# Attention and MLP on one core: the diagonals of the softmax sums move off GpSimd, and their product with ones moves in TensorE's order

## The chip, the cores and the metric

The kernel runs on one core of one Trainium2 chip. A core has TensorE (PE in the profile; PEld is its weight load), VectorE (DVE), ScalarE (ACT), GpSimd (POOL) and SyncE (SP), each with an instruction queue of its own that it works off in order, and DMA engines that move data between HBM and on-chip memory. The metric is the device time of one execution, in microseconds. Lower is better.

## The reference

Sliding-window attention with four sink positions, then a two-layer MLP. All inputs are float32.

```python
# q, k, v: [4, 8, 768, 64] (batch, heads, sequence, head size); 4 sinks, window 128
scores = matmul(q, k.T) / sqrt(64)
keep   = (pos_k < 4) | ((0 <= pos_q - pos_k) & (pos_q - pos_k < 128))
scores = where(keep, scores, -1e9)
a      = exp(scores - max(scores))
a      = a / (sum(a) + 1e-9)
x      = matmul(a, v)                        # then [3072, 512]: heads side by side
h      = x @ w_in                            # [512, 2048]
g      = where(h >= 1, h, where(h <= -1, 0, (h + 1)**2 / 4))
out    = g @ w_out                           # [2048, 512]
```

The factors on q and k (about 30) make the softmax sharp, so that the scores need float32's precision.

## The kernel before

**Tiles and chunks.** A unit is 384 query positions (CT = 3 tiles of 128) of one head of one batch; there are 64. Eight units, the heads of one batch and one half of the sequence, make a chunk, whose rows are then 384 tokens of the MLP. The program records steps: the attention of one chunk is interleaved (`spread`) with the MLP of the chunk before. TensorE keeps the recorded order (`manual_schedule` for PE). On the other engines a scheduler that goes by a modelled timeline sets the order, so that a change at one place moves instructions elsewhere too.

**Two kinds of attention.** The first 16 units (NATIVE) are worked in 8 pairs of heads, with float32 matmuls (`pair_*`). The other 48 go one by one with values split in two parts of a shorter format (`scores`, `transp`, `av`); the change doesn't touch these. Nor does it touch the MLP (`stage1`, `stage2`), which has split values too.

**A pair.** For pair m, `pair_scores(m, i)` multiplies q by k for query tile i and both heads, adds the mask and takes the maximum on VectorE (line 388), and makes exp on ScalarE (line 393), which also sums each row into `stat`. After the third tile (line 395 on), the sums are finished: 1e-9 is added on GpSimd (line 396), VectorE takes the reciprocal (397), and GpSimd multiplies the identity by it, a column of 128 per query tile (400): `diag` is three diagonal matrices of 128 x 128 beside each other, and lives in a buffer named q_l. One step later `pair_r` multiplies `diag` by a matrix of ones (437), which puts one over the sum of each query into every row of a PSUM bank; ScalarE copies that into `xn` (438). `early_transp` turns the unnormalized p (408, 410) and ScalarE copies it out (411, 412, 414). `pair_av` multiplies it by v (427), and VectorE multiplies the result by `xn` (430). So the division comes last, and no instruction ahead of `pair_av` needs `diag`.

**Steps.** `pair_steps(m)` holds what belongs to pair m and to pair m - 1 at once: three scores of pair m (sc), four half transposes of pair m - 1 (tp: both parts of head a, then of head b), then the product with ones and p times v of pair m - 1 (pv). For m that is a multiple of 4 the order of these differs a little. In what follows, step m is this list; step 4 has pair 4's scores and pair 3's p times v. Steps 0 to 4 are the first chunk, with no MLP beside them but the decoding of four weight tiles; steps 5 to 8 are interleaved with the first chunk's MLP and the decoding of the other twelve.

**Decoding.** The weights come as 64-bit words of float64 (lines 150 to 156). VectorE puts the bits together with three instructions (150, 153, 154), ScalarE rounds to the high part (155), VectorE subtracts for the rest (156). 16 tiles (8 of `w_in`, 8 of `w_out`) of 1 MB each are loaded by SyncE's queue, later by ScalarE's (173).

**PSUM.** `ps_a` has three banks, which scores, transposes, the product with ones and p times v share in turn.

Of the kernel before, what the change touches and what calls it, by code (L numbers as in the profile page):

```python
# [12 lines left out]
AF = mybir.ActivationFunctionType  # L13
ALU = mybir.AluOpType

B, H, S, D = 4, 8, 768, 64
DM, DFF = 512, 2048
P = 128
NT = S // P
CT = 3  # L20
# [29 lines left out]
def attn_ffn(ctx, tc, qk, qkp, vx, vs, par, w_in, w_out, out):  # L50
    nc = tc.nc
# [10 lines left out]
    ident = const.tile([P, P], F32, name="ident")  # L62
# [57 lines left out]
    for r0 in (0, 32):  # L120
        r = r0 + CT * NSINK
# [226 lines left out]
    def pair_load(m):  # L348

        b, h, _ = units[2 * m]  # L350
        T = CT * P
        W = CT * KB - NSINK
        q_s = att.tile([P, T], F32R, name="q_h").bitcast(F32)
        k_s = att.tile([P, P + CT * KB], F32R, name="k_s").bitcast(F32)[:, :W]
        loaded.append(nc.sync.dma_start(k_s, qkp[b, h // 2, :, T:T + W]).ins)
        nc.sync.dma_start(q_s, qkp[b, h // 2, :, 0:T])
        st["qk", m] = q_s, k_s

    def pair_values(m):
        v_s = vq[m % 2]  # L360
        for a in range(2):
            b, h, _ = units[2 * m + a]
            nc.sync.dma_start(v_s[:, :CT, a], vx[b, h, :, :CT])
            nc.sync.dma_start(v_s[:NSINK, CT, a], vs[b, h, :NSINK])

    def early_p(u):

        return (p0[u % 2] if u // 2 % 2 == 0 else pt0[u % 2][:, 5 * P:5 * P + CT * 260]).rearrange(
            "p (i c) -> p i c", c=260)

    def pair_scores(m, i):
        q_s, k_s = st["qk", m]
        lo, c0 = (KB if i == 0 else 0), max(0, (i - 1) * KB)
        banks = []
        for a in range(2):

            pool, name = ((ps_o, "o_ps"), (ps_o, "o_ps"), (ps_o, "o_ps"), (ps_h, "h_ps"), (ps_h, "h_ps"),
                          (ps_a, "ps_a"))[2 * i + a] if m <= H // 2 - 1 else (ps_a, "ps_a")
            ps = pool.tile([P, 512], F32, name=name)
            r = slice(a * D, a * D + D)  # L380
            nc.tensor.matmul(ps[:, lo:260], lhsT=q_s[r, i * P:(i + 1) * P], rhs=k_s[r, c0:c0 + 260 - lo],
                             start=True, stop=True)
            banks.append(ps)
        for a, ps in enumerate(banks):
            u = 2 * m + a
            p = early_p(u)[:, i, lo:260]
            peak_i = peak[:, u, i:i + 1]
            nc.vector.tensor_tensor_reduce(out=p, in0=ps[:, lo:260], in1=(m0, m1n, m2)[i], scale=-0.125, scalar=3.0e38,
                                           op0=ALU.add, op1=ALU.min, accum_out=peak_i)
            if not i:  # L390
                st["sum", u] = att.tile([P, 2 * CT], F32, name=f"stat{a}")
            stat = st["sum", u]
            nc.scalar.activation(p, p, AF.Exp, bias=peak_i, scale=-1.0, accum_out=stat[:, i:i + 1])
            if i == CT - 1:

                nc.gpsimd.tensor_scalar(stat[:, CT:2 * CT], stat[:, 0:CT], 1.0e-9, None, op0=ALU.add)
                nc.vector.reciprocal(stat[:, CT:2 * CT], stat[:, CT:2 * CT])  # L397
                diag = st["diag", u] = att.tile([P, CT * P], F32R, name="q_l").bitcast(F32)
                for n in range(CT):
                    nc.gpsimd.tensor_scalar(diag[:, n * P:(n + 1) * P], ident, stat[:, CT + n:CT + n + 1], None,  # L400
                                            op0=ALU.mult)

    def early_transp(u, part):

# [27 lines left out]
    def pair_r(m):  # L432

        T = CT * P
        ps = ps_a.tile([P, 512], F32, name="ps_a")
        for a in range(2):
            nc.tensor.matmul(ps[a * D:a * D + D, :T], lhsT=ones, rhs=st.pop(("diag", 2 * m + a)), start=True, stop=True)  # L437
        nc.scalar.copy(xn[:, units[2 * m][1] // 2, :], ps[:, :T])

    def pair_steps(m):  # L440

        a, b = 2 * m - 2, 2 * m - 1
        sc = [(0.45, lambda i=i: pair_scores(m, i)) for i in range(CT)] if m < NATIVE // 2 else [(0.0, lambda: None)] * CT
        steps = [(0.0, lambda: pair_load(m + 1))] if m + 1 < NATIVE // 2 else []
        if m < NATIVE // 2:
            steps.append((0.0, lambda: pair_values(m)))
        if not m:
            return [(0.0, lambda: pair_load(0))] + steps + sc
        tp = [(0.35, lambda u=u, i=i: early_transp(u, i)) for u in (a, b) for i in range(2)]
        pv = [(0.65, lambda: pair_r(m - 1)), (1.2, lambda: pair_av(m - 1))]  # L450
        if m % (H // 2) == 0:
            return steps + tp[:3] + sc[:1] + pv[:1] + tp[3:] + sc[1:2] + pv[1:] + sc[2:]
        return steps + tp[:1] + sc[:1] + tp[1:3] + pv[:1] + tp[3:] + sc[1:2] + pv[1:] + sc[2:]

# [195 lines left out]
    with tc.If(other_v > 0):  # L652
        with tc.tile_pool(name="gen", bufs=1) as gen:

            for n in range(2 * NJ):
# [3 lines left out]
                m = gen.tile([P, DM], F32, name="m")  # L659
# [3 lines left out]
            for t0 in (0, CT):  # L663
                keep = gen.tile([P, CT, S], F32, name="keep")
                kidx = gen.tile([P, S], I32, name="kidx")
                r = gen.tile([P, S], F32, name="r")
                for i in range(CT):
                    m = keep[:, i]
# [53 lines left out]
```

## Time and profile before

| | |
|---|---|
| median of 3 runs | 761.11 us (760.46 to 762.45) |
| the profiled execution | 761.86 us |
| its span, first to last instruction | 759.9 us |
| mean granted TensorE clock | 0.973 |
| busy: TensorE, VectorE, ScalarE, GpSimd | 708.2, 517.0, 492.2, 357.8 us |

A row of a group of instructions reads: line, engine, operation, tile written <- tiles read, shapes, count | busy us, mean ns of one | idle us of the engine ahead of them, and what ended it. A row of the waits reads: who waited <- for whom: us in total, times, longest. A row of the table by stages reads: stretch in us from the start, its length, each engine's busy time with its count of instructions, granted TensorE clock, share of the DMA engines, GB/s. A row of the timeline reads: start, duration, engine, line, operation, tiles, shapes, count [idle before it <- what ended that]. A row of the chain reads: start, duration, engine, tile, line, count. A row on one line of the kernel gives the shortest, the median and the longest duration in ns.

### The profile page before, as it was taken

What the parts mean: (1) busy time and instruction counts of PE and PEld (TensorE: products, weight loads), DVE (VectorE), ACT (ScalarE), POOL (GpSimd) and SP (SyncE); (2) the same over time, 40 slices, a digit from 0 to 9 for tenths busy, and PEclk for the clock granted to TensorE, in tenths of its full rate; (3) what the DMA queues carried; (4) which work ended last, traced back from release to release, by engine and by line L of the source; (5) the groups of instructions that cost most, each with busy time, mean ns of one, the idle gap of its engine ahead of it and who ended that gap; (6) DMA issues with size and microseconds to landing.
All of it is one profiled execution on the core that took longest, in us unless ns stands there. A gap on an engine that the chain in (4) does not pass through costs nothing.

```text
span 759.9 us, 12272 instructions
## 1 busy us (share of the span) xinstructions
PE 708.2 (93%) x3873; PEld 613.0 (81%) x3873; DVE 517.0 (68%) x1321; ACT 492.2 (65%) x1265; POOL 357.8 (47%) x578
## 2 busy tenths in 40 slices
PE   4667997889999999999999999999999999999996
PEld 2234765678999899999988999899988999999985
DVE  6345877666877678777878778787888677742221
ACT  3445655466777787778877787678867676644342
POOL 5334547657545255564656555564656455410000
PEclk9768998999999999999999999999999999999999
DMA  7714333131313253333333344333332121001001
GB/s 224 232 47 166 137 136 122 66 103 43 97 54 107 69 151 114 117 120 134 117 97 115 85 143 141 95 120 132 117 93 65 53 87 46 9 1 43 1 0 47
DMA packets 44841, 73.04 MB, mean 96 GB/s; under 512 B 13024, under 2 KB 29408, under 8 KB 44768
## 3 DMA queue, kind: packets, MB, share of 16 engines
q1 hardware_dynamic: 41504, 59.59, 25.8%
q10 hardware_dynamic: 3264, 12.58, 4.6%
q8 instruction: 33, 0.54, 0.3%
q14 instruction: 40, 0.33, 0.1%
HBM read 65.87 MB, written 6.29 MB: 95 GB/s over the span
## 4 chain that ended last, share of the span: by engine, by line
PE 68%; POOL 9%; DVE 9%; issue 5%; DMA 4%; ACT 4%; SPq 0%; POOLq 0%; ACTq 0%
PE o_ps L503 27%; PE h_ps L484 27%; POOL q_l L400 6%; PE ps_a L342 4%; PE ps_a L240 4%; PE ps_a L295 2%; PE ps_a L427 1%; PE ps_a L437 1%; DVE k_s L224 1%; DMA w<-w_in 1%; DVE p L259 1%; POOL gl L495 1%; POOL q_l L226 1%; DVE gl L495 1%; DVE bits L153 1%
## 5 line engine op out<-in xcount | busy, mean ns | idle before, releaser
L484 PE MATMUL h_ps<-x,wi 128*128 128x384 f32 x1536 | 311.1, 341 | 1.3 <-DVE g L493 1.3
L484 PEld LDWEIGHTS h_ps<-x,wi 128*128 128x128 f32 x1536 | 264.1, 189 | 13.0 <-issue 3.3
L503 PE MATMUL o_ps<-w,gh 128*128 128x512 f32 x768 | 245.1, 400 | 0.4 <-ACT gh L494 0.4
L503 PE MATMUL o_ps<-w,gl 128*128 128x512 f32 x384 | 152.1, 396 | 0.4 <-POOL gl L495 0.4
L503 PEld LDWEIGHTS o_ps<-w,gh 128*128 128x128 f32 x768 | 135.0, 189 | 17.5 <-issue 2.0
L493 DVE SCALAR_TENSOR_TENSOR g<-g,h_ps 128x384 f32<-128x384 f32 x128 | 70.2, 549 | 65.5 <-ACT g L492 64.7
L491 ACT ACTIVATE g<-h_ps,half 128x384 f32<-128x384 f32 x128 | 73.8, 577 | 62.4 <-PE h_ps L484 62.1
L226 POOL TENSOR_TENSOR q_l<-r,q_h 128x384 fp32r<-128x384 f32 x48 | 50.1, 1043 | 128.1 <-ACT q_h L225 111.2
L494 ACT CAST gh<-g 128x384 fp32r<-128x384 f32 x128 | 65.5, 512 | 55.7 <-DVE g L493 54.8
L503 PEld LDWEIGHTS o_ps<-w,gl 128*128 128x128 f32 x384 | 72.5, 189 | 18.6 <-POOL gl L495 0.8
L495 DVE TENSOR_TENSOR gl<-g,gh 128x384 fp32r<-128x384 f32 x112 | 69.2, 618 | 24.4 <-ACT gh L494 23.4
L247 ACT ACTIVATE p<-p,peak 128x260 f32<-128x260 f32 (+1 forms) x144 | 71.3, 496 | 15.2 <-DVE peak L244 14.3
L224 DVE TENSOR_TENSOR k_s<-k_r,k_s 64x524 fp32r<-64x524 f32 (+1 forms) x44 | 47.1, 1071 | 43.5 <-ACT k_s L222 43.4
L244 DVE CUSTOM_DVE_ANT_0 p<-ps_a,m 128x260 f32<-128x260 f32 (+1 forms) x144 | 57.3, 409 | 17.1 <-PE ps_a L240 16.0
L492 ACT ACTIVATE g<-g 128x384 f32<-128x384 f32 x128 | 67.0, 524 | 2.6
L306 POOL TENSOR_SCALAR_AFFINE_SELECT pt<-pt 128x384 fp32r<-128x384 f32 (+1 forms) x96 | 50.8, 529 | 24.5 <-DVE pt L299 21.3
L304 POOL TENSOR_SCALAR_AFFINE_SELECT pt<-pt 128x384 fp32r<-128x384 f32 (+1 forms) x96 | 51.5, 537 | 7.2 <-ACT pt L298 3.2
L259 DVE TENSOR_SCALAR p<-p,stat 128x132 f32<-128x132 f32 (+1 forms) x144 | 51.6, 412 | 0.1
L400 POOL TENSOR_SCALAR q_l<-ident,stat 128x128 f32<-128x128 f32 x48 | 47.2, 998 | 4.2 <-DVE stat L397 2.8
L342 PEld LDWEIGHTS ps_a<-pt,v_s 128*128 128x128 f32 x304 | 46.4, 188 | 2.3
L342 PE MATMUL ps_a<-pt,v_s 128*128 128x256 f32 (+1 forms) x304 | 46.7, 273 | 0.0
L240 PE MATMUL ps_a<-k_s,q_h 128*128 128x260 f32 (+1 forms) x144 | 40.1, 279 | 3.2 <-DVE sk L301 2.4
(148 smaller groups left out, 1033.7 us busy)
## 6 DMA issues: line engine op xcount, KB each, us to landing
r<-qk SPq DMA_DIRECT2D x48, 192.0 KB
k_r<-qk SPq DMA_DIRECT2D x32, 262.0 KB
again<-w_in SPq DMA_DIRECT2D x16, 512.0 KB
again<-w_out SPq DMA_DIRECT2D x16, 512.0 KB
w<-w_in ACTq DMA_DIRECT2D x6, 1024.0 KB
w<-w_out ACTq DMA_DIRECT2D x6, 1024.0 KB
out<-o SPq DMA_DIRECT2D x23, 256.0 KB
r<-vx SPq DMA_DIRECT2D x32, 128.0 KB
```

The costliest lines, as they stand in the source:

```text
L240: nc.tensor.matmul(ps[:, lo:260], lhsT=q[:, i * P:(i + 1) * P], rhs=k_s[:, c0:c0 + 260 - lo], start=(j == 0), stop=(j == len(qs) - 1))
L247: nc.scalar.activation(p[:, i, lo:260], p[:, i, lo:260], AF.Exp, bias=peak_i, scale=-1.0, accum_out=stat[:, i:i + 1])
L259: nc.vector.tensor_scalar(p[:, i, lo:260], p[:, i, lo:260], stat[:, CT + i:CT + i + 1], None, op0=ALU.mult)
L342: nc.tensor.matmul(z, lhsT=w, rhs=y, start=(n == 0), stop=(n == len(mms) - 1))
L400: nc.gpsimd.tensor_scalar(diag[:, n * P:(n + 1) * P], ident, stat[:, CT + n:CT + n + 1], None, op0=ALU.mult)
L484: nc.tensor.matmul(h_ps[:, :T], lhsT=w_i[j][:, w, ct * P:(ct + 1) * P], rhs=x[:, y, ct], start=(ct == 0 and n == 0), stop=(ct == NCT - 1 a ...
L491: nc.scalar.activation(g, h_ps[:, :T], AF.Relu, bias=half, scale=0.5)
L492: nc.scalar.activation(g, g, AF.Square)
L493: nc.vector.scalar_tensor_tensor(g, g, 1.0, h_ps[:, :T], op0=ALU.min, op1=ALU.max)
L494: nc.scalar.copy(gh, g)
L495: (nc.gpsimd if row0 == GL_POOL else nc.vector).tensor_tensor(gl, g, gh.bitcast(F32), op=ALU.subtract)
L503: nc.tensor.matmul(o_ps[tt], lhsT=gg[:, tt * P:(tt + 1) * P], rhs=w_o[j][:, w], start=(j == 0 and n == 0), stop=(j == NJ - 1 and n == 2))
```

## The change

The addition of 1e-9 moves from GpSimd to VectorE. For pairs 0 to 3, VectorE makes the three diagonals of a head in one instruction, the identity and the reciprocals being read broadcast. For pairs 4 to 7, ScalarE makes them, as three copies with a scale. In TensorE's order the product with ones is put behind the last transpose, and outside of steps 4 and 8 behind the second score too.

```diff
             if i == CT - 1:
 
-                nc.gpsimd.tensor_scalar(stat[:, CT:2 * CT], stat[:, 0:CT], 1.0e-9, None, op0=ALU.add)
-                nc.vector.reciprocal(stat[:, CT:2 * CT], stat[:, CT:2 * CT])
+                r = stat[:, CT:2 * CT]
+                nc.vector.tensor_scalar(r, stat[:, 0:CT], 1.0e-9, None, op0=ALU.add)
+                nc.vector.reciprocal(r, r)
                 diag = st["diag", u] = att.tile([P, CT * P], F32R, name="q_l").bitcast(F32)
-                for n in range(CT):
-                    nc.gpsimd.tensor_scalar(diag[:, n * P:(n + 1) * P], ident, stat[:, CT + n:CT + n + 1], None,
-                                            op0=ALU.mult)
+                if m < H // 2:
+                    nc.vector.tensor_tensor(diag.rearrange("p (i q) -> p i q", q=P),
+                                            ident.unsqueeze(1).broadcast_to([P, CT, P]),
+                                            r.unsqueeze(2).broadcast_to([P, CT, P]), op=ALU.mult)
+                else:
+                    for n in range(CT):
+                        nc.scalar.activation(diag[:, n * P:(n + 1) * P], ident, AF.Copy, scale=r[:, n:n + 1])
...
         if m % (H // 2) == 0:
-            return steps + tp[:3] + sc[:1] + pv[:1] + tp[3:] + sc[1:2] + pv[1:] + sc[2:]
-        return steps + tp[:1] + sc[:1] + tp[1:3] + pv[:1] + tp[3:] + sc[1:2] + pv[1:] + sc[2:]
+            return steps + tp[:3] + sc[:1] + tp[3:] + pv[:1] + sc[1:2] + pv[1:] + sc[2:]
+        return steps + tp[:1] + sc[:1] + tp[1:] + sc[1:2] + pv + sc[2:]
```

The new lines move those behind them: line numbers from 400 on grow by 5 (408 becomes 413, 437 becomes 442, 427 becomes 432, 430 becomes 435, 484 becomes 489).

TensorE in step 2, before: the second part of head a's transposes, the first of head b's, the product with ones, then the second part of head b's, the scores of tile 1, and p times v (vq is v, spn the sinks' part of p).

```order
L408 MATMUL ps_a<-ident,pt 128x128 x2
L410 MATMUL ps_a<-ident,pt 4x128
L408 MATMUL ps_a<-ident,pt 128x128 x3
L437 MATMUL ps_a<-q_l,ones 64x384 x2
L408 MATMUL ps_a<-ident,pt 128x128 x2
L410 MATMUL ps_a<-ident,pt 4x128
L381 MATMUL o_ps<-k_s,q_h 128x260
L381 MATMUL h_ps<-k_s,q_h 128x260
L427 MATMUL ps_a<-pt,vq_166 64x128 x2
```

And now:

```order
L413 MATMUL ps_a<-ident,pt 128x128 x2
L415 MATMUL ps_a<-ident,pt 4x128
L413 MATMUL ps_a<-ident,pt 128x128 x5
L415 MATMUL ps_a<-ident,pt 4x128
L381 MATMUL o_ps<-k_s,q_h 128x260
L381 MATMUL h_ps<-k_s,q_h 128x260
L442 MATMUL ps_a<-q_l,ones 64x384 x2
L432 MATMUL ps_a<-pt,vq_166 64x128 x2
```

The product with ones (L437, now L442) has gone behind three transposes and two scores, and stands directly ahead of p times v.

VectorE in the same step, before: from the softmax of the last tile of pair 1's second head to the first softmax of pair 2's tile 1 (ISA is the mask with its maximum, and the read of the maximum; bits are the words being decoded).

```order
L388 ISA pt_178,peak_97<-ps_a_312,m2_106 128x260
L388 ISA peak_97 128x1
L397 RECIPROCAL stat0_257<-stat0_257 128x3
L388 ISA p_175,peak_97<-o_ps_343,m0_109 128x128
L388 ISA peak_97 128x1
L154 SCALAR_TENSOR_TENSOR bits1_304<-w_203,bits1_304 128x1024
L388 ISA p_176,peak_97<-o_ps_345,m0_109 128x128
L388 ISA peak_97 128x1
L397 RECIPROCAL stat1_260<-stat1_260 128x3
L156 TENSOR_TENSOR w_303<-bits1_304,w_303 128x2x512
L388 ISA p_175,peak_97<-o_ps_374,m1n_108 128x260
```

And now, from the two additions on:

```order
L397 TENSOR_SCALAR stat0_253<-stat0_253 128x3
L397 TENSOR_SCALAR stat1_256<-stat1_256 128x3
L154 SCALAR_TENSOR_TENSOR bits1_300<-w_203,bits1_300 128x1024
L388 ISA p_175,peak_97<-o_ps_362,m1n_108 128x260
L388 ISA peak_97 128x1
L398 RECIPROCAL stat0_253<-stat0_253 128x3
L398 RECIPROCAL stat1_256<-stat1_256 128x3
L388 ISA p_176,peak_97<-h_ps_364,m1n_108 128x260
L388 ISA peak_97 128x1
L401 TENSOR_TENSOR q_l_314<-ident_79,stat0_253 128x384
L401 TENSOR_TENSOR q_l_320<-ident_79,stat1_256 128x384
L156 TENSOR_TENSOR w_299<-bits1_300,w_299 128x2x512
```

The two diagonals now stand behind the third decode instruction and the softmax of both heads' tile 1.

ScalarE at the start of the MLP, now (L496 is the first activation of an MLP tile, L419, L416 and L417 copy transposes out):

```order
L393 ACTIVATE p,stat_529<-p,peak 128x260
L173 DMA w<-w_out 128x2x1024
L393 ACTIVATE pt,stat_618<-pt,peak 128x128
L393 ACTIVATE pt,stat_621<-pt,peak 128x128
L406 ACTIVATE q_l<-ident,stat_526 128x128 x3
L406 ACTIVATE q_l<-ident,stat_529 128x128 x3
L496 ACTIVATE g<-h_ps,half 128x384
L416 COPY pt<-ps_a 128x256
```

The six diagonals of pair 4 (L406) stand between two exponentials of pair 5 and the first MLP activation, which before followed the exponentials directly.

## The prediction

> **What bounds the kernel now.** I began with the page: the busy shares, the chain of work that ended last, and the group on GpSimd's diagonals.
>
> ```profile
> PE 708.2 (93%) x3873; PEld 613.0 (81%) x3873; DVE 517.0 (68%) x1321; ACT 492.2 (65%) x1265; POOL 357.8 (47%) x578
> PEclk9768998999999999999999999999999999999999
> PE o_ps L503 27%; PE h_ps L484 27%; POOL q_l L400 6%; PE ps_a L342 4%; PE ps_a L240 4%; PE ps_a L295 2%; PE ps_a L427 1%; PE ps_a L437 1%; DVE k_s L224 1%; DMA w<-w_in 1%; DVE p L259 1%; POOL gl L495 1%; POOL q_l L226 1%; DVE gl L495 1%; DVE bits L153 1%
> L400 POOL TENSOR_SCALAR q_l<-ident,stat 128x128 f32<-128x128 f32 x48 | 47.2, 998 | 4.2 <-DVE stat L397 2.8
> ```
>
> TensorE is busy for 93% of the span, so only the missing 7%, some 50 us, and the time at a low clock can be won. GpSimd's 47.2 us of diagonals are mostly on the chain (6% of the span, some 42 us), though GpSimd as a whole is the least busy engine. Next, by stage, the waits of TensorE (first up to 72 us, then 72 to 190 us), and the table of stages, cut where TensorE begins a pair:
>
> ```profile
> PE ps_a L437 <- POOL q_l L400: 17.8, 8, 3.7
> PE ps_a L437 <- POOL q_l L400: 8.7, 5, 2.9
> PE h_ps L484 <- DVE g L493: 1.3, 1, 1.3
> core 0: us, PE busy (x) PEld busy (x) DVE busy (x) ACT busy (x) POOL busy (x), PEclk, DMA share, GB/s
> 8.66:24.16 15.50, 10.93 (x45) 5.17 (x45) 7.99 (x27) 7.76 (x27) 6.11 (x9) 1.00 0.71 230
> 24.16:40.93 16.77, 9.74 (x46) 4.43 (x44) 7.23 (x22) 6.73 (x22) 7.13 (x9) 0.69 0.71 226
> 40.93:57.24 16.31, 10.41 (x47) 4.74 (x45) 7.22 (x21) 6.70 (x22) 6.57 (x8) 0.69 0.14 37
> 57.24:71.67 14.43, 9.68 (x46) 4.69 (x44) 7.96 (x21) 6.93 (x22) 5.73 (x8) 0.76 0.33 106
> 71.67:160.20 88.53, 78.52 (x418) 58.77 (x419) 62.37 (x108) 49.62 (x121) 50.44 (x48) 0.96 0.35 122
> 190.00:720.00 530.00, 526.49 (x2971) 480.80 (x2970) 389.27 (x1033) 379.44 (x975) 256.54 (x442) 1.00 0.30 90
> ```
>
> Two stages carry the case. From 8.7 to 71.7 us four pairs run alone (steps 1 to 4): no engine is full, and each step is one chain. From 71.7 to 160 us four more pairs run between the first chunk's MLP matmuls: TensorE is nearly full there and waits 8.7 us for the diagonals. Behind 190 us TensorE is full, and no instruction of the change is left; I put that part at nothing. The timeline of step 2 shows the chain:
>
> ```profile
> 28.49 2.79 POOL L400 TENSOR_SCALAR q_l<-ident,stat 128x128 f32<-128x128 f32 x3 [0.51 <-DVE stat L397]
> 31.33 1.54 PE L437 MATMUL ps_a<-q_l,ones 128*64 128x384 f32 x2 [3.70 <-POOL q_l L400]
> 31.97 2.58 POOL L400 TENSOR_SCALAR q_l<-ident,stat 128x128 f32<-128x128 f32 x3 [0.38 <-DVE stat L397]
> 34.60 1.54 PE L437 MATMUL ps_a<-q_l,ones 128*64 128x384 f32 x2 [1.73 <-POOL q_l L400]
> 38.08 2.07 PE L427 MATMUL ps_a<-pt,vq 128*64 128x128 f32 x12
> 39.98 0.39 PE L427 MATMUL ps_a<-spn,vq 128*64 128x128 f32 x4
> ```
>
> Behind the second product with ones stand two transposes, two scores and p times v, in TensorE's order; the next step begins behind these.
>
> **The change part by part.** Removed from GpSimd: 48 diagonals and 16 additions. TensorE's eight products with ones move behind work that doesn't need them. VectorE gets 16 additions, and 8 products of 128x384 for pairs 0 to 3; ScalarE gets 24 products of 128x128 for pairs 4 to 7. The trace has no such instruction on these engines; the nearest rows, with those of the chain that the new step has to run through:
>
> ```profile
> 5.42 0.16 DVE L78 TENSOR_SCALAR big<-par_f 128x2 f32<-128x2 f32 x1
> 13.30 1.22 DVE L154 SCALAR_TENSOR_TENSOR bits<-w,bits 128x1024 int32<-128x1024 int32 x1
> 23.20 0.39 PE L427 MATMUL ps_a<-spn,vq 128*64 128x128 f32 x4
> 38.18 0.43 DVE L388 CUSTOM_DVE_ANT_0 p<-o_ps,m1n 128x260 f32<-128x260 f32 x1 [5.26 <-PE h_ps L381]
> 40.44 0.56 DVE L430 TENSOR_TENSOR xn<-ps_a,xn 128x384 f32<-128x384 f32 x1 [1.48 <-PE ps_a L427]
> 40.92 0.68 DVE L150 TENSOR_SCALAR bits<-w 128x1024 int32<-128x1024 int32 x1
> 41.86 0.55 DVE L515 TENSOR_TENSOR x<-xn,x 128x384 fp32r<-128x384 f32 x1
> 43.82 0.17 DVE L397 RECIPROCAL stat<-stat 128x3 f32<-128x3 f32 x1
> 43.90 0.26 DVE L388 CUSTOM_DVE_ANT_0 pt<-o_ps,m 128x128 f32<-128x128 f32 x1
> 60.65 0.40 ACT L393 ACTIVATE p<-p,peak 128x128 f32<-128x128 f32 x1 [0.19 <-DVE peak L388]
> 67.43 1.24 PE L381 MATMUL ps_a<-k_s,q_h 64*128 64x260 f32 x4
> 107.91 1.30 PE L427 MATMUL ps_a<-pt,vq 128*64 128x128 f32 x12
> 109.04 0.39 PE L427 MATMUL ps_a<-spn,vq 128*64 128x128 f32 x4
> L412 ACT COPY spn<-ps_a x16: 240/249/250, 13.8 to 155.2; 4x128 f32<-4x128 f32 x16
> ```
>
> An addition is 0.16 us (the 128x2 row). A VectorE diagonal is 0.55 (L515, the same size out of SBUF; an operand that is read broadcast could make it cheaper, not below the 0.26 of the 128x128 row, nor above the 1.22 of a 128x1024 one). A ScalarE diagonal lies between 0.25 (the 4x128 copy) and 0.40 (the 128x128 exponential); nearer the latter, 0.35.
>
> *Steps 2 and 3.* From the end of one p times v to the next, the new chain is VectorE's queue up to the second diagonal, in the new order, and TensorE behind it. The queue: xn 0.56, first decode instruction 0.68, two softmax parts 0.86, split of x 0.55, second decode instruction 1.22 (as the L154 row), two 128x128 softmax parts 0.52, two additions 0.32, third decode instruction 1.22, softmax part, two reciprocals, softmax part (0.43 + 0.34 + 0.43), two diagonals 1.10: 8.2 us. Then the second product with ones, 0.77 (half of the 1.54), and p times v, 2.30 (38.08 to 40.37): 11.3 us. Transposes and scores, which stood behind the product, now pass under the queue. With TensorE at full clock the two end terms are 0.43 (half of 0.86, below) and 1.52 (107.91 to 109.43): 10.2 us. I take 10.8, the middle. No engine is over that: VectorE's 7.2 busy plus 1.4 added are 8.6, ScalarE stays at 6.7. Today the two steps last 16.8 and 16.3 us (the table's third and fourth row): 6.0 and 5.5 are saved.
>
> *Step 1.* The third decode instruction started at 13.30. Two additions ahead of it: 13.62 to 14.84; reciprocals 0.34, diagonals 1.10: 16.3; second product 0.77, p times v 2.3: 19.4, against 23.6 now (the end of the 23.20 row). Saved: 4.2.
>
> *Step 4.* The diagonals stand ahead of the decode in VectorE's queue: xn 0.56, softmax 0.86, x 0.55, then 0.16 + 0.17 + 0.55, 0.16, 0.26, 0.17, 0.55: 4.0, and about 0.7 for the exponential between (longer than the 0.40 row, for 260 columns). Then the second product 0.77, two pairs of scores 1.24, p times v 2.3, and an allowance of 0.5 for PSUM banks that must be emptied first: 9.5 against 14.4. Saved: 4.9.
>
> Sum of the first stage: 20.6 us. Ends: 17 if TensorE stays cold and steps 2 to 4 lose another 1 us each to a late copy or softmax; 24 with TensorE at full clock in all. Loads are covered: SyncE's list moves the next pair's k and q ahead of a small load of v, both a whole step before their use; and the weights of this stage have landed by step 3, where the DMA moves 37 GB/s after 226 at 0.71 of its engines. Without that cover a late load would stand at the decode, and the lower end would hold it.
>
> *Pairs 4 to 7.* The waits of 8.7 go, since the diagonals come several MLP matmuls ahead of the product. With them goes slow work behind the longest wait:
>
> ```profile
> 122.64 0.86 PE L437 MATMUL ps_a<-q_l,ones 128*64 128x384 f32 x2 [1.20 <-POOL q_l L400]
> 126.36 1.54 PE L437 MATMUL ps_a<-q_l,ones 128*64 128x384 f32 x2 [2.86 <-POOL q_l L400]
> 127.90 4.12 PE o_ps L503 x9
> 148.40 0.86 PE L437 MATMUL ps_a<-q_l,ones 128*64 128x384 f32 x2 [1.80 <-POOL q_l L400]
> 152.44 2.07 PE o_ps L503 x9
> ```
>
> The same nine matmuls took 4.12 us there and 2.07 elsewhere (both from the chain), the same product 1.54 and 0.86: 2.7 more. At most 11.4. ScalarE gets 24 x 0.35 = 8.4 us and is then at 58 of some 78 us; VectorE gets 8 additions, 1.3 us, and is at 64 of 78, 82%. Both are in-order, and the ScalarE diagonals wait for reciprocals; behind them in ScalarE's queue stands the first MLP activation, for which the second layer waits two tiles later. Today's 1.3 us wait for g shows that this cover is nearly used up at the start of the stage. I take 2 us off: 9.4. Ends: 5 and 11.4. If the cover were gone, all 8.4 us of ScalarE's diagonals would show: 3.0.
>
> Total: 20.6 + 9.4 = 30.0 us. The profiled execution has 759.9 us of span in 761.86 us; it becomes 731.9. The median, 761.11, becomes **731 us**.
>
> Where TensorE's clock stands in steps 1 to 4 is open. A product behind waits of 2.86 and more ran cold, one behind 1.80 or less at full clock, so this trace puts the limit between. The new step has some 2 us between the last score and the product, which falls just there; hence the middle above. The Trainium skill, "TensorE: Matmul & The Clock Gate", Part 1, "What's actually happening", has the clock fall to half after an idle window of about 3.4 us, a window that runs on its own. The 2.86 us wait, with a cold product behind it, has the trace fall earlier than that; by the page, the new steps would all be warm.
>
> **The rivals.**
>
> *Warm throughout.* If the gaps stay under TensorE's limit, steps 2 and 3 take 10.2 (6.6 and 6.1 saved), and steps 1 and 4 lose another 1.1 each (0.34 + 0.78: 5.3 and 6.0 saved): 24.0; the second stage gives its 11.4. 35.4 us: 726 us. The page of the Trainium skill named above would have it come out this way. For it: cold work is now 0.69 of the clock in steps 2 and 3. Against it: the 2.86 row.
>
> *The wait changes its name.* Products with ones now wait for VectorE: the diagonals stand behind two decode instructions and two softmax parts that themselves wait for scores and PSUM banks. If each step loses 2.4 us more to that (two decode instructions run through ahead of late operands), the first stage gives 20.6 - 9.6 = 11.0, the second, with VectorE at 82%, the lower end, 5: 16 us saved, 745 us. For it: softmax and decode share one in-order queue, and VectorE waited 5.3 us for scores in one go. Against: those waits were behind the very product that now goes first.
>
> *Slower: ScalarE's queue stands.* In pairs 4 to 7 a diagonal on ScalarE that waits for its reciprocal holds all MLP activations behind it, and through them TensorE. The reciprocal waits in VectorE's queue, where one decode is 0.68 + 3 x 1.22 = 4.3 us. With a stall s per pair the stage pays 4 s + 8.4 and the change still has 20.6 + 11.4 = 32.0 to give: it is slower from s = 5.9 us on. Two decodes ahead of the reciprocal, 8.7 us, make 43.2: 772 us. For it: two in-order queues, one waiting on the other. Against: the new VectorE order has the reciprocals ahead of the decode at the first of these pairs, and two MLP tiles lie between an activation and its use.
>
> *Nothing moved.* The product is late for another reason and the time stays at 761 us. Against: the two rows name GpSimd's diagonals in all 13 waits.
>
> **How the numbers follow.** Forecast 0.60 (its own range, by the ends of both stages, 24 + 11.4 and 17 + 5: 726 to 739); warm 0.17; changed wait 0.18; slower 0.03; nothing 0.02. The range takes in the warm case and most of the changed wait: 723 to 744. This kernel's runs can't tell under 0.3% (2.3 us) from no change. Faster 0.95, no change 0.02, slower 0.03.
>
> **What would show it.** Right: no wait of TensorE for GpSimd in the first 160 us; the chain names VectorE's third decode, reciprocals and diagonals; steps of 10 to 11.5 us; the first MLP matmul near 51 us, not 72; VectorE's diagonals at 0.55 us, ScalarE's at 0.35; the matmuls from then to the first native scores in some 79 us. Wrong: products with ones that wait over 1 us for VectorE or ScalarE, steps over 13 us, 1.54 us products still behind short gaps, or new waits for g or weights in the second stage.

## The result, and the profile after

The changed kernel takes 725.46 us, the median of four executions, of which three lie between 721.03 and 726.67 us; the fourth, at 1133.8 us and a granted clock of 0.561, was disturbed, as was one of the six of e3_vector below (766.85 us, 0.848), and neither is part of a ratio. The kernel before took 760.97 us beside it. The ratio is 0.9511, with a 95% interval of 0.9462 to 0.956: some 37 us, or 4.9%, are gone. Six further executions of the same kernel gave 723.72 us and a ratio of 0.9507 (0.948 to 0.9534). The profiled execution took 724.25 us with a span of 722.5 us, against 761.86 and 759.9 before.

From the page of the kernel after, the busy shares, the granted clock and the chain by line:

```profile
PE 691.1 (96%) x3873; PEld 609.8 (84%) x3873; DVE 530.1 (73%) x1345; ACT 496.4 (69%) x1289; POOL 304.7 (42%) x514
PEclk9899999999999999999999999999999999999999
PE 73%; DVE 15%; ACT 6%; DMA 2%; issue 2%; POOL 1%; SPq 0%; ACTq 0%; DVEq 0%; POOLq 0%
```

GpSimd, which was 6% of the chain with its diagonals alone, is 1% of it in all; TensorE is busy for 17 us less, although it does the same matmuls, because fewer of them run at the low clock and, as shown below, because some run at the same time. Next, the waits of TensorE, first up to 49 us and then from 49 to 127 us:

```profile
PE ps_a L442 <- DVE q_l L401: 5.1, 2, 2.6
PE ps_a L442 <- ACT spn L417: 0.9, 1, 0.9
```
```profile
PE h_ps L489 <- DVE g L498: 1.0, 1, 1.0
PE ps_a L240 <- DVE peak L244: 0.4, 1, 0.4
```

Before, GpSimd held the product with ones 13 times for 26.5 us. It no longer does so at all. VectorE now holds it twice, in steps 2 and 3, for 2.56 us each. In step 1 the product waits 0.9 us for a copy out of `ps_a` on ScalarE (L417), and in step 4 for nothing. The table by stages, cut where TensorE begins a pair:

```profile
8.66:19.00 10.34, 8.50 (x49) 5.38 (x51) 9.54 (x31) 7.77 (x27) 0.00 (x0) 1.00 0.85 273
19.00:29.55 10.55, 7.23 (x46) 4.96 (x48) 8.15 (x26) 6.94 (x24) 0.63 (x2) 0.84 0.85 295
29.55:39.90 10.35, 6.99 (x44) 4.75 (x44) 8.01 (x27) 6.62 (x23) 0.00 (x0) 0.84 0.60 199
39.90:47.16 7.26, 5.97 (x41) 3.45 (x41) 6.91 (x22) 5.71 (x21) 0.00 (x0) 1.00 0.30 80
47.16:121.40 74.24, 73.25 (x419) 56.67 (x420) 64.80 (x115) 55.23 (x146) 23.01 (x16) 1.00 0.45 154
```

The four steps now take 10.3, 10.6, 10.4 and 7.3 us (15.5, 16.8, 16.3 and 14.4 before), and the second stage 74.2 instead of 88.5, with TensorE busy for all but 1 us of it. In exact ends: the last matmul of p times v in steps 1 to 4 ended at 23.59, 40.37, 56.56 and 70.99 us, and now at 17.82, 28.36, 38.75 and 45.88. The first MLP matmul starts at 47.47 us (71.98). The second stage ends where the first score of the other kind of attention starts (line 240; the prediction calls it a native score, but the NATIVE units are the pairs): at 121.48 us (160.48).

So the sum is: 25.1 us from the first stage (70.99 - 45.88), 0.6 lost between it and the first MLP matmul, 14.5 from the second (88.50 - 74.01), and 1.6 lost behind it; together the 37.4 us by which the span is shorter. The small loss at the end is seen in TensorE's waits behind that point, first before (from 160 us), then after (from 121 us), then in a second profiled execution of the changed kernel (after_again, from 121.56 us):

```profile
PE ps_a L240 <- DVE sk L301: 2.4, 3, 1.3
```
```profile
PE ps_a L240 <- DVE sk L301: 3.9, 5, 1.4
```
```profile
PE ps_a L240 <- DVE sk L301: 2.4, 3, 1.4
```

In that second execution the part behind the second stage takes 599.3 us, as it did before the change (599.4); in the first it takes 601.0. So the 1.6 us belong to the execution, and are not shown to be a cost of the change.

Step 2 as the chain of waits of the kernel after shows it (start, duration, engine, tile, line, count):

```profile
17.93 0.56 DVE xn L435
...
20.25 1.14 DVE bits L153
...
21.95 1.13 DVE bits L154
23.08 0.34 DVE p L388
...
23.43 0.15 DVE stat L398 x2
23.58 0.32 DVE p L388
...
23.90 0.48 DVE q_l L401
24.39 0.14 issue
24.52 1.73 PE ps_a L442 x4
26.25 2.13 PE ps_a L432 x13
```

It is VectorE's queue from the end of one p times v to the first diagonal, and then TensorE alone. The prediction had it run to the second diagonal; that one is ready at 24.84 us, while the product of the first head is already running. The costs of the new instructions, from the groups of the first 160 us (busy us, mean ns of one, idle before):

```profile
L401 DVE TENSOR_TENSOR q_l<-ident,stat 128x384 f32<-128x384 f32 x8 | 4.2, 553 | 0.1
L397 DVE TENSOR_SCALAR stat<-stat 128x3 f32<-128x3 f32 x16 | 2.2, 159 | 0.0
L406 ACT ACTIVATE q_l<-ident,stat 128x128 f32<-128x128 f32 x24 | 7.5, 392 | 0.0
```

### The profile page after: what moved, and what is told of

Its sections match the earlier page's. It is cut to its first block, busy times and chain, and to the rows that moved or that the text cites. A ratio compares the mean times of both kernels' runs of the same rounds, so it can differ in the third digit from the quotient of the medians.

```text
span 722.5 us, 12238 instructions
## 1 busy us (share of the span) xinstructions
PE 691.1 (96%) x3873; PEld 609.8 (84%) x3873; DVE 530.1 (73%) x1345; ACT 496.4 (69%) x1289; POOL 304.7 (42%) x514
## 4 chain that ended last, share of the span: by engine, by line
PE 73%; DVE 15%; ACT 6%; DMA 2%; issue 2%; POOL 1%; SPq 0%; ACTq 0%; DVEq 0%; POOLq 0%
PE o_ps L508 30%; PE h_ps L489 29%; PE ps_a L342 4%; PE ps_a L240 4%; PE ps_a L295 2%; DVE k_s L224 2%; DVE p L259 1%; DVE bits L153 1%; PE ps_a L432 1%; DVE g L498 1%; DMA w<-w_in 1%; DVE gl L500 1%; ACT p L247 1%; DVE p L256 1%; DMA r<-qk 1%
## 5 line engine op out<-in xcount | busy, mean ns | idle before, releaser
L489 PEld LDWEIGHTS h_ps<-x,wi 128*128 128x128 f32 x1536 | 263.6, 189 | 11.5 <-issue 1.5
L508 PEld LDWEIGHTS o_ps<-w,gh 128*128 128x128 f32 x768 | 134.3, 189 | 17.7 <-issue 2.8
L496 ACT ACTIVATE g<-h_ps,half 128x384 f32<-128x384 f32 x128 | 73.9, 577 | 59.1 <-PE h_ps L489 58.0
L508 PEld LDWEIGHTS o_ps<-w,gl 128*128 128x128 f32 x384 | 72.2, 188 | 17.8
L259 DVE TENSOR_SCALAR p<-p,stat 128x132 f32<-128x132 f32 (+1 forms) x144 | 54.4, 431 | 0.1
L500 POOL TENSOR_TENSOR gl<-g,gh 128x384 fp32r<-128x384 f32 x16 | 21.9, 1370 | 68.4 <-ACT gh L499 60.5
```

The costliest lines, as they stand in the source:

```text
L259: nc.vector.tensor_scalar(p[:, i, lo:260], p[:, i, lo:260], stat[:, CT + i:CT + i + 1], None, op0=ALU.mult)
L489: nc.tensor.matmul(h_ps[:, :T], lhsT=w_i[j][:, w, ct * P:(ct + 1) * P], rhs=x[:, y, ct], start=(ct == 0 and n == 0), stop=(ct == NCT - 1 a ...
L496: nc.scalar.activation(g, h_ps[:, :T], AF.Relu, bias=half, scale=0.5)
L500: (nc.gpsimd if row0 == GL_POOL else nc.vector).tensor_tensor(gl, g, gh.bitcast(F32), op=ALU.subtract)
L508: nc.tensor.matmul(o_ps[tt], lhsT=gg[:, tt * P:(tt + 1) * P], rhs=w_o[j][:, w], start=(j == 0 and n == 0), stop=(j == NJ - 1 and n == 2))
```

## The experiments

Two theories stood against each other at first: that the time came from GpSimd leaving the chain, with TensorE's new order as a cover for what waits remain; or that the new order alone would have hidden the slow diagonals. After that each part was sized by itself. All times are medians, with the ratio to the kernel before that ran beside it; the table gives the length of steps 1 to 4 (the first as the end of its p times v), and the second stage from the first MLP matmul to the first score of the other kind, each in the profiled execution, in us.

| kernel | median | ratio (95% interval) | step 1 | 2 | 3 | 4 | second stage |
|---|---|---|---|---|---|---|---|
| before | 761.11 | 1 | 23.6 | 16.8 | 16.2 | 14.4 | 88.5 |
| the change | 725.46 | 0.9511 (0.9462 to 0.956) | 17.8 | 10.5 | 10.4 | 7.1 | 74.0 |
| after_again | 723.72 | 0.9507 (0.948 to 0.9534) | 17.6 | 10.8 | 10.5 | 7.1 | 74.0 |
| e1_order | 749.45 | 0.9841 (0.982 to 0.9862) | 22.4 | 14.0 | 14.3 | 14.4 | 80.4 |
| e2_engines | 734.69 | 0.9643 (0.9621 to 0.9665) | 20.9 | 12.8 | 11.4 | 7.8 | 78.2 |
| e7_twice | 733.42 | 0.9634 (0.9615 to 0.9652) | 19.2 | 14.0 | 13.2 | 8.2 | 74.3 |
| e3_vector | 722.99 | 0.9489 (0.9459 to 0.9518) | 17.7 | 9.2 | 9.6 | 7.1 | 73.8 |
| e4_scalar | 735.02 | 0.9639 (0.9609 to 0.967) | 21.9 | 12.0 | 13.0 | 10.7 | 73.9 |
| e5_warm | 722.42 | 0.9479 (0.9451 to 0.9507) | 17.7 | 9.2 | 9.5 | 7.1 | 74.0 |
| e6_apart | 728.48 | 0.9559 (0.9533 to 0.9585) | 17.4 | 10.4 | 10.5 | 7.5 | 78.0 |
| e9_ahead | 725.28 | 0.9521 (0.9497 to 0.9545) | 20.4 | 10.7 | 8.2 | 9.7 | 74.2 |
| e11_later | 724.01 | 0.9498 (0.9474 to 0.9521) | 19.6 | 6.2 | 10.3 | 11.0 | 74.6 |
| e10_both | 722.74 | 0.9504 (0.9478 to 0.953) | 17.4 | 9.2 | 9.4 | 7.1 | 73.7 |

**The change once more**, for more executions beside the first experiments:

> The changed kernel once more, as the measure for the runs beside it. Its executions so far lay between 721.0 and 726.7 us, with mean clocks of 0.993 to 0.990 in that order. Theory of the clock: the same spread, the longer the lower the clock, because TensorE's gap ahead of the product in steps 2 and 3 (2.56 us) lies at the limit where the clock falls. Rival: one time within 0.3%, the spread being chance of those runs.

723.72 us, as above, with executions from 721.17 to 728.33 us. The shortest has the highest granted clock (0.995) and the longest the lowest (0.988), but the four between them, all at 0.990, still differ by 1.9 us. The theory of the clock is borne out at the ends, and no more. The two profiled executions of this kernel reach the end of the second stage at 121.48 and 121.56 us, both with slow products in steps 2 and 3; the 1.7 us between their spans lie behind it.

**The order alone** (the kernel before with the new list of steps):

```diff
-            return steps + tp[:3] + sc[:1] + pv[:1] + tp[3:] + sc[1:2] + pv[1:] + sc[2:]
-        return steps + tp[:1] + sc[:1] + tp[1:3] + pv[:1] + tp[3:] + sc[1:2] + pv[1:] + sc[2:]
+            return steps + tp[:3] + sc[:1] + tp[3:] + pv[:1] + sc[1:2] + pv[1:] + sc[2:]
+        return steps + tp[:1] + sc[:1] + tp[1:] + sc[1:2] + pv + sc[2:]
```

> The new order of TensorE alone, additions and diagonals on GpSimd as before. Theory (the diagonals' duration on GpSimd sets the first stage): each of steps 1 to 4 keeps GpSimd's 5.6 us and gains only what now passes under it, two transposes and two scores (2.0 us), less 0.4 as both heads' products start cold together: 4 x 1.6 = 6.5 us; pairs 4 to 7 lose about two thirds of their 8.7 us of waits, 2 of cold matmuls, and 3.2 as the two heads' products run at the same time: 11. Together some 744 us. Rival (it was the place of the product, not the engine): 725 to 730 us.

749.45 us: 12.3 below the 761.78 of the kernel before that ran with it, where 744 us were expected. The first stage gained 5.9 us in the profiled execution (6.5 expected), the second 8.2 (11 expected). TensorE's waits in it, up to 66 us and from 66 to 146 us:

```profile
PE ps_a L437 <- POOL q_l L400: 11.8, 7, 2.4
```
```profile
PE ps_a L437 <- POOL q_l L400: 4.5, 2, 3.3
```

The order hides 6.0 of the 17.8 us of waits in the first stage and 4.2 of the 8.7 in the second, and no more (the rest of the second stage's 8.2 us is a TensorE that is busy for 75.8 instead of 78.5 us, and the wait for g, which is gone): GpSimd's diagonals were on the chain, not merely issued in an unlucky place.

**The engines alone** (the change with the old list of steps, the same four lines the other way round):

> The new engines alone, the product with ones in its old place in TensorE's order. Theory: in steps 1 to 3 transposes and scores of 2.0 us stand behind the product on the chain again, while the product comes some 0.9 us earlier, since VectorE makes the diagonals ahead of the softmax of tile 1: 1.1 to 1.6 us a step, 4 us in all, pairs 4 to 7 unchanged: 728 to 730 us. Rival (the place of the product carries the gain): 740 us and more, nearer the kernel before.

734.69 us, 27.1 below 761.78, so two thirds of the change and more. The two halves, 12.3 and 27.1, come to 39.4 against 38.1 for both together: they are nearly independent. TensorE's waits, up to 54 us, and from 54 to 132:

```profile
PE ps_a L442 <- DVE q_l L401: 7.8, 3, 2.8
```
```profile
PE ps_a L413 <- ACT pt L393: 2.1, 1, 2.1
```

With the old order VectorE's diagonals are waited for longer, and work that could run meanwhile stands behind. The kernel came out 5 us slower than expected. Of the 11 us by which it is behind the change, 6.9 are in the first stage, and 4.2 in the second (78.2 against 74.0), where TensorE waits 2.1 us for an exponential and is busy for 75.4 instead of 73.0 us, with a granted clock of 0.98 instead of 1.00.

**VectorE's diagonals written twice**, for pairs 0 to 3:

```diff
-                    nc.vector.tensor_tensor(diag.rearrange("p (i q) -> p i q", q=P),
+                    for _ in range(2):
+                        nc.vector.tensor_tensor(diag.rearrange("p (i q) -> p i q", q=P),
```

> VectorE writes each diagonal of pairs 0 to 3 twice, the same values. Theory: VectorE's queue up to the diagonals is the chain of steps 1 to 3, so each step grows by one diagonal ahead of the first product and one more behind (0.55 to 1.1 us a step): 2 to 4 us over the changed kernel. Rival (the product waits for something else, such as copies on ScalarE, and the diagonals are covered): within 0.5 us of it.

It cost 9.7 us, where 2 to 4 were expected. In steps 1 and 4 the dose shows at about its size (1.4 and 1.1 us for two more instructions of 0.5), in steps 2 and 3 it costs 3.5 and 2.8. The chain of waits there says why:

```profile
15.76 6.20 DMA vs_r<-vs
...
21.99 0.03 ACT vsx L277
...
22.14 0.52 ACT x L520
...
22.68 0.56 DVE x L521
...
26.89 0.94 DVE q_l L402 x2
27.83 1.14 DVE w L156
28.97 0.48 DVE q_l L402
```

The scheduler put the decode's last instruction (L156, 1.14 us) ahead of the last of the four diagonals, and put ScalarE's copy of a small load ahead of the rounding of x, so that x waited for that load (3.46 us from p times v to x, 1.96 in the change). 0.96 for the dose, 1.14 and 1.5 come to 3.6 us, for 3.5 measured. The experiment shows that VectorE's queue is the path of steps 2 and 3, but not the price of a diagonal in it: the reordering cost more than the instructions.

**One engine for all diagonals.** VectorE:

```diff
-                if m < H // 2:
+                if True:
```

> VectorE makes all diagonals, ScalarE none. Theory: among the MLP matmuls TensorE is busy for 73.3 of 74.2 us, so it does not matter which engine makes the diagonals of pairs 4 to 7: within 1.5 us of the changed kernel. Rival 1 (ScalarE's 24 diagonals, 7.5 us, delay the MLP activations): 3 to 7 us faster than it. Rival 2 (VectorE, at 65 of 74 us there, is the next bound): 3 us slower or more.

And ScalarE:

```diff
-                if m < H // 2:
+                if False:
```

> ScalarE makes all diagonals, VectorE only additions and reciprocals. Theory: in steps 1 to 4 the six diagonals of a pair take 1.9 us on ScalarE against 1.0 on VectorE, but they no longer stand in VectorE's queue; ScalarE is the less busy (6.6 to 7.8 us a step, VectorE 8 to 9.5). The product waits for the last of them: 0.4 to 0.9 us a step, 1.5 to 3.5 us slower than the changed kernel. Rival (VectorE's load, not its queue's end, sets the step): 1 us a step faster, 3 to 4 us.

VectorE for all: 722.99 us, not to be told from the change, as expected. The second stage is 73.8 us instead of 74.0, so that either engine has room for eight diagonals there. ScalarE for all: 735.02 us, 11 more than the change, where 1.5 to 3.5 were expected. ScalarE in step 1 (timeline), and in step 3 (chain):

```profile
14.94 1.04 ACT L155 CAST wi<-bits 128x1024 fp32r<-128x1024 f32 x1
15.89 1.86 ACT L406 ACTIVATE q_l<-ident,stat 128x128 f32<-128x128 f32 x6
```
```profile
39.17 1.02 ACT wi L155
...
40.59 0.88 ACT q_l L406 x3
```

The copies themselves are short, 1.86 us for the six of a pair. But they stand behind the decode's rounding (L155), which can only follow VectorE's third decode instruction. The product of step 1 began at 16.97 us instead of 15.29, and at the low clock (1.73 us for three of its matmuls, 0.91 in the change). So what VectorE saves by it comes back through ScalarE's queue. In step 4 (10.7 us for 7.1) the chain runs through that queue too, through the diagonals, the copies out and the exponentials. In the second stage, 73.9 us, it again makes no difference. The choice of engine matters only in the first stage, and there because of what stands ahead of the diagonals in the queue.

**The gap filled**: ten matmuls of ones by the identity, overwritten afterwards, ahead of the product with ones in steps 2 and 3.

```diff
+        for _ in range(10 if m in (1, 2) else 0):
+            nc.tensor.matmul(ps[:D, :P], lhsT=ones, rhs=ident, start=True, stop=True)
         for a in range(2):
```

> In steps 2 and 3, ten small matmuls of ones by the identity go ahead of the product, into the bank that the product then overwrites; they do nothing but fill TensorE's gap of 2.56 us. Theory (the clock falls in that gap): both products take 0.9 instead of 1.7 us and p times v 1.5 instead of 2.1, 1.4 us a step, 2.8 us in all; the spread of the times shrinks. Rival (these matmuls are slow for another reason, such as late operands): no gain, or a loss of up to 1 us a step where the filling runs longer than the gap.

In the profiled execution steps 2 and 3 fell from 10.5 and 10.4 to 9.2 and 9.5 us, and the first MLP matmul to 45.16 us. That is the size that was expected, but one execution doesn't show that the filling did it: e3_vector has steps of 9.2 and 9.6 us with the gap left open. The median, 722.42 us, is lower than the change's 723.72 by less than the intervals can tell.

**The two heads' products apart**, in pairs 4 to 7: one directly ahead of the second score, the other behind it.

```diff
+            ra, rb = [(0.325, lambda h=h: pair_r(m - 1, (h,))) for h in range(2)]
...
+            return steps + tp[:1] + sc[:1] + tp[1:] + [ra] + sc[1:2] + [rb] + pv[1:] + sc[2:]
```

> For pairs 4 to 7, head a's product with ones stands ahead of the scores of tile 1 and head b's behind them, both long after their diagonals are ready. Theory (the products of the two heads, which fill 64 columns each, run at the same time when they are issued together, and one after the other when apart): 0.86 us more a pair, 3 to 3.5 us in all. Rival (the second stage's gain beyond 11.4 us came from elsewhere): within 1 us of the changed kernel.

728.48 us, 4.8 more than the change, though the intervals of the two ratios just touch. The second stage is 4.0 us longer, with TensorE busy for 77.0 instead of 73.0 us and the same 1.0 us of wait for g. The stage is the better measure here: the profiled execution, 723.98 us, is the shortest of the six, because the part behind the stage took only 596.9 us in it. The product in it, then in the change (timeline; the count tells one head, x2, from both, x4):

```profile
55.34 0.86 PE L444 MATMUL ps_a<-q_l,ones 128*64 128x384 f32 x2
60.14 0.86 PE L444 MATMUL ps_a<-q_l,ones 128*64 128x384 f32 x2
```
```profile
57.81 0.87 PE L442 MATMUL ps_a<-q_l,ones 128*64 128x384 f32 x4
```

Two heads in a row take as long as one; four products of 0.86 more are 3.4 of the 4.0 us. That is a part of the gain that the prediction had not seen.

**The diagonals ahead of the third decode instruction**, by a hold on that instruction and with the decoding recorded a little later (0.9), or later still (0.85):

```diff
+        with tc.issue_after(st["last"].ins) if pin and "last" in st else nullcontext():
+            nc.vector.scalar_tensor_tensor(w, low, 29, w, op0=ALU.logical_shift_right, op1=ALU.bitwise_or)
...
-                    nc.vector.tensor_tensor(diag.rearrange("p (i q) -> p i q", q=P),
+                    st["last"] = nc.vector.tensor_tensor(diag.rearrange("p (i q) -> p i q", q=P),
...
-        for _, f in spread(attn, prev, LEAD if c else 1.0):
+        for _, f in spread(attn, prev, LEAD if c else 0.9):
```

> The changed kernel, but the third decode instruction is held behind the last diagonals recorded ahead of it, with the decoding recorded a little later; in VectorE's order this moves step 3 alone: the two diagonals now come ahead of the third decode instruction there. Theory (the chain through VectorE's queue sets the step): the 1.12 us of that instruction leave the chain, step 3 takes 9.3 instead of 10.4 us with TensorE cold behind the gap, and some 8.3 if the now shorter gap leaves it at full clock; steps 2 and 4 as in the change; the median 1 to 2 us below the change, little against its spread, so the step's length decides. Rival (step 3 is held by scores or exponentials as much as by the decode): step 3 stays within 0.4 us of 10.4.

> The same hold with the decoding recorded later still: step 2 has no third decode instruction and no first or second ahead of its diagonals, step 3 has the rest of one decode and two instructions of the next ahead of its diagonals. Theory (VectorE's queue sets steps 2 and 3): step 2 falls from 10.5 to between 7.0 and 7.8 us, as step 4 with its 7.1 has no decode either; step 3 stays at 10 to 11; the first MLP matmul near 44.5 us instead of 47.5; the median near 721. Rival (the decode then comes too late): the time shows again as TensorE's wait for weights at the start of the second stage, and the median stays at 724 or above.

In the first, step 3 fell to 8.2 us, as the theory had it for a TensorE at full clock; in the second, step 2 to 6.2. Neither kernel is faster: 725.28 and 724.01 us, where 1 to 2 us below the change and 721 us were expected. In the first, what step 3 gained, step 4 lost (9.7 instead of 7.1). The chain of the first of the two, at the end of step 3:

```profile
38.48 0.95 ACT wi L156
...
39.46 1.23 DVE wi L157
40.68 0.48 DVE xn L436
```

Rounding and subtraction of the decode, held back by 1.1 us and more, now stand ahead of the product by `xn` with which the next step begins. Two thirds of the loss of the second kernel lie in the same place (step 4 takes 11.0 us); the rest is step 1, which in both of these executions ran at the low clock. Weights that come too late are not the cause: in the second stage of the second kernel TensorE waits only 1.1 us, for g. Three decodes have to pass through VectorE in these steps, and it only matters in part where.

**Both edits together**, VectorE for all diagonals and the gap filled:

> VectorE makes all diagonals, and ten more matmuls of ones by the identity (their result is overwritten) stand ahead of the product with ones in steps 2 and 3. Theory: both edits alone were within 1 to 2 us of the change; together steps 2 and 3 take 9.2 to 9.6 us in every execution, since the gap that lets TensorE's clock fall is filled; the profile then reads like that of either edit, the first MLP matmul near 45.2 us, the median near 722, and the executions lie closer together than the change's 721 to 728. Rival (the clock in steps 2 and 3 has no part in the spread between executions): the same median, but a spread of 6 us or more.

722.74 us. Steps of 9.2 and 9.4 us, the first MLP matmul at 44.8 us: the profile is what was expected. The executions lie between 721.3 and 726.8 us, with granted clocks of 0.996 to 0.990, those of the filled gap alone between 720.0 and 724.1 with 0.994 to 0.996, those of the change between 721.2 and 728.3 with 0.988 to 0.995. That is no clear answer: 5.4 us of spread against the 6 that would have spoken against the clock decide nothing. The longest execution again has the low 0.990, with the gap filled. No kernel here is faster than the change by more than the intervals can tell.

## Why the prediction was right, and where its terms were not

The forecast was 731 us in a range of 723 to 744; the median is 725.46, the gain of the span 37.4 us instead of 30.0. In steps 2 and 3 and in the second stage the mechanism was the one described, and the rows that were to show it are there: no wait for GpSimd, a chain that names the third decode, the reciprocals and a diagonal, steps 2 and 3 of 10.5 and 10.4 us for a forecast of 10.8, no wait for a diagonal in the second stage. In steps 1 and 4 the path was another, as said below. Some signs came out otherwise: step 4 took 7.1 us and not 10 to 11.5, the first MLP matmul came at 47.5 us and not near 51, the second stage took 74 us and not 79. One of the signs of being wrong is there too, a wait of more than 1 us for VectorE; it should not have been among them, since the prediction's own steps end in that queue. "The wait changes its name" came true in kind (5.1 us for VectorE) but not in price, since it had been counted: the steps were worked out from that queue. "Slower: ScalarE's queue stands" did not happen; the MLP's only wait in that stage is the same 1.0 us for g.

Both stages gave more than the value taken, by 4.5 and 5.1 us; the 2.2 lost between and behind them in this execution, which were in no term, leave the 7.4 us by which the gain exceeds the forecast. The rival "Warm throughout" came nearer to the median with its 726 us, but not by its mechanism: steps 2 and 3 were to be warm, and ran cold.

*Steps 1 and 4* hold 4.0 of the first 4.5. Step 1 saved 5.8 instead of 4.2: the second diagonal was ready at 15.6 us, not 16.3, and the product and p times v behind it took 2.2 us, not 3.1, at full clock. Step 4 saved 7.3 instead of 4.9: the second diagonal was ready 4.1 us into it instead of 4.7, and from there to the end of p times v it took 3.0 us, where the product, the scores, p times v and the allowance for PSUM banks had been put at 4.8. In neither step did VectorE's queue set the time alone: in step 1 the first product waited for a copy on ScalarE (L417), and in step 4 the product started right behind the transposes, at 42.72 us, with no wait for a diagonal. The rival "Warm throughout" had 5.3 and 6.0 for these two steps; they ran warm, as it said, while steps 2 and 3 ran cold.

*Steps 2 and 3* were right by luck: by errors that cancel in part, and by a middle. The 10.8 us lie between a sum of 11.3 for a cold TensorE and one of 10.2 for a warm one; TensorE was cold, and the steps took 10.5 and 10.4. The queue up to the second diagonal was put at 8.2 us and measured 6.9 (17.93 to 24.84). The instructions cost what was said, but a row's duration holds about 0.08 us in which the next one is already running. VectorE in step 2 of the kernel after:

```profile
21.87 1.22 DVE L154 SCALAR_TENSOR_TENSOR bits<-w,bits 128x1024 int32<-128x1024 int32 x1
23.00 0.42 DVE L388 CUSTOM_DVE_ANT_0 p<-o_ps,m1n 128x260 f32<-128x260 f32 x1
```

1.22 us from 21.87 would end at 23.09, and the next begins at 23.00. Over the 17 instructions of this queue that makes the 1.3 us. In the other direction, the part of the product with ones that remained behind the second diagonal was put at 0.77 us and took 1.41 (24.84 to 26.25).

*The term that failed is that 0.77*, "half of the 1.54", and with it the 2.7 us of slow work in the second stage. The row of 1.54 us with the count x2 is one head's, and I read it as both heads', although step 2 has two such rows. At the low clock both heads together take 1.73 us, so nothing like a half of one row remains; in the second stage, where the change puts both heads' products behind one another without a wait between, the second is free. The kernel before showed it, in a row that I passed over, and in the sums of the groups, first of the kernel before (71.67 to 160.2 us), then of the change (47.16 to 121.4 us):

```profile
80.17 0.87 PE L437 MATMUL ps_a<-q_l,ones 128*64 128x384 f32 x4
```
```profile
L437 PE MATMUL ps_a<-q_l,ones 128*64 128x384 f32 x16 | 6.7, 557 | 8.7 <-POOL q_l L400 8.7
```
```profile
L442 PE MATMUL ps_a<-q_l,ones 128*64 128x384 f32 x16 | 3.5, 512 | 0.0
```

6.7 to 3.5 us: of these 3.2 only 0.7 was in a term, as the cold product. With the waits (8.7, and 0.3 less for g) and 2.05 for the nine slow MLP matmuls the second stage adds up to 14.25 us, and 14.5 were measured. The upper end of 11.4 could not reach that, and the 2 us taken off for VectorE and ScalarE were not called for: both engines had room. The heads' products kept apart cost 4.0 us in the same stage, which bears out this term.

*The part behind 190 us* was put at nothing. In the first profiled execution 1.6 us were lost behind the second stage, in the second one nothing (601.0 and 599.3 us, 599.4 before). This trailing part differs between the experiments too (722.3 us of span less 125.41 leave 596.9 in e6_apart), and what sets it was not settled.

## What to carry to other kernels

Where a wait on a slow engine is removed, follow the queue that is then last, in its new order, and price it by starts, not by durations: the next start less this start is what an instruction costs its queue. Read the count in a row before halving or doubling it; the same work in pieces of one and of two may differ twofold. And moving work off the chain of one step is worth nothing while the next step has to take it up: measure the sum of the steps, not the step.

## What was not expected of the hardware

**Two heads' products at the same time.** Each product uses 64 of the columns of TensorE's array (128*64 in its row) and writes its own half of the bank. Back to back, the two take 0.87 us at full clock, as one does alone (0.86). The Trainium skill, "TensorE: Matmul & The Clock Gate", Part 3, "Packing small matmuls — row/col tiling", says that matmuls on separate parts of the array run concurrently; the rows here agree.

**The same gap, once cold and once warm.** The product with ones of step 2, in the change and in the kernel with VectorE for all diagonals, and that of step 1 in the kernel with the third decode held back:

```profile
24.52 1.92 PE L442 MATMUL ps_a<-q_l,ones 128*64 128x384 f32 x4 [2.56 <-DVE q_l L401]
```
```profile
24.41 0.92 PE L442 MATMUL ps_a<-q_l,ones 128*64 128x384 f32 x3 [2.56 <-DVE q_l L401]
25.17 0.49 PE L442 MATMUL ps_a<-q_l,ones 128*64 128x384 f32 x1
```
```profile
15.90 1.92 PE L443 MATMUL ps_a<-q_l,ones 128*64 128x384 f32 x4 [0.53 <-ACT spn L418]
```

TensorE's matmuls ahead of the first two are the same, and so is the gap of 2.56 us; all of it lies 0.1 us earlier in the second. One execution is cold behind it, the other not, and the third is cold behind 0.53 us: the five transposes ahead of it had been slow already, 1.69 us against 1.27 in the change (and 0.71 in its step 2), so no fall in that gap is needed. The prediction's limit "between 1.80 and 2.86" is therefore no limit of a gap's length, and its own row at 34.60 us, cold behind 1.73 us and behind a cold product, already spoke against it. Something else comes in; the position in time would fit. The Trainium skill, "TensorE: Matmul & The Clock Gate", Part 1, "What's actually happening", has the activity watched in windows of about 3.4 us that run freely, which fits two outcomes of one gap; that only a whole idle window makes the clock fall does not fit a cold product behind 2.56 us. The price is small: 0.8 to 1.3 us in each of steps 2 and 3. That this is part of the change's spread from 721 to 728 us is not shown: the two profiled executions are both cold there, and what they differ by, 1.7 us, lies behind the second stage.

**The granted clock in the table by stages** reads 1.00 in the first steps of a run even where the durations are those of the low clock, as in step 1 with the order alone (first the table, then the timeline):

```profile
8.66:22.41 13.75, 11.05 (x42) 5.91 (x42) 7.64 (x25) 7.34 (x26) 5.98 (x8) 1.00 0.74 238
```

```profile
15.83 1.54 PE L437 MATMUL ps_a<-q_l,ones 128*64 128x384 f32 x2 [0.80 <-POOL q_l L400]
```

In the first steps the durations tell, not that column.
